# Moving four small copies to GpSimd, one normalisation ahead of a transposition, and splitting the last product: windowed attention with a gated MLP on one Trainium2 core

## The chip, the core and the metric

The kernel runs on one core of a Trainium2 chip. A core has a matrix engine (TensorE, in the profile PE, with its weight loads as PEld), a vector engine (VectorE, DVE), an activation engine (ScalarE, ACT), a general engine (GpSimd, POOL) and a queue engine (SyncE, SP), which here issues the DMAs. Each engine works through its own instructions in order and waits on semaphores for the others. Matrix products land in PSUM, all else lies in SBUF. The metric is the device time of one execution in microseconds (us).

## The reference

There are 8 batches, 8 heads, 576 positions and heads of 64. First comes attention in which each position sees itself and the 63 before it; then a gated MLP over the 512 joined columns, whose gate mixes positions.

```
scores = 0.125 * q @ k.T;  mask: 0 <= i - j < 64
attn   = softmax(scores) @ v             # then heads joined: x is (8, 576, 512)
h      = relu(x @ w_in);  u, v = h[..., :512], h[..., 512:]
v_n    = (v - mean(v)) / sqrt(var(v) + 1e-6)
v_s    = w_spatial @ v_n + b_spatial     # over positions
out    = (u * v_s) @ w_out               # float32
```

## The kernel before

The program is built of small named steps. Each step is a function that emits the instructions of one piece of work; a long string, `ORDER`, lists all steps in the order of emission, each with its engine (`DQ` is SP's DMA queue) and with the numbers of the buffers that it takes: `tk2_0:DVE:2`. Nothing else decides the order: an engine's instructions come in the order in which its steps stand in the list, and a step that waits holds up all that stands behind it on its engine. Semaphores between engines follow from which step writes and reads which part of a tile. PSUM has two pairs of banks (0 and 1) for scores and four single banks, which the list numbers 0 to 3 as well; a product can begin only when its bank has been read by the step that used it last.

A step's name has a letter or two, the batch, an underscore and what part of it. For batch b, head group g (0 or 1, four heads each) and half u of a group:

- `ldq`, `ldk`, `ldv`: loads by SP into the tiles nq, nk, nv. `cq`, `ck`: cast to float16 (hq, hk); on POOL three instructions of 384 columns. `tq`, `tk`: transposition by DVE (line 408) into qT, kT.
- `cv{b}_{g}{n}`: cast of V into hv (line 301 on POOL for batches 0 and 1, in two parts n = 0 and 1; from batch 2 on in one step with two instructions, line 299). P needs V at two offsets of 64 positions, so there is a second tile, hs, shifted by 64 partitions: `sl` copies the lower half of the partitions of hv to it, `su` the upper half, `s4` the last 64 positions from nv. These are the small copies of V; each is 64 partitions by 512 (256 for part 0 of `sl`).
- `S`: scores (line 470). `E`: exponential on ACT (477). `M`: the mask as a minimum on DVE (480, and 553 for the last 64 positions, marked r). `Z`: row sums as a product with ones (493). `N` and `n`: logarithm of the sum and exponential of its negative on ACT (519, 521), giving lz, the inverse. `P`: product with V from hv and hs (504). `X`: the normalisation, P's bank times lz, on DVE into x (512).
- `V` and `U`: the two halves of x @ w_in (643, 698; 656 and 703 for the last positions). `Vr`, `Ur`: relu on ACT (623, 711). `Vb`, `Va`: statistics on DVE (625, 627); `L1`, `L2`: inverse deviation on ACT (670, 672). `A`: v_n on DVE (682). `G`: product with w_spatial (728, 734). `Ge`: times u, on DVE (742). `O`: product with w_out (753). `Oe`: copy from the bank to ob by ACT (606). `st`: store by SP (610, 613, 616).
- `W`, `We`: transposition of w_spatial on PE (368) and the copy of it to SBUF; `cwo`, `cwin`, `cwsp`: casts of weights.

The batches are a pipeline: while batch 0 goes through the MLP, batch 1 is in attention and batch 2 is being loaded. The last 64 positions of out (`O{b}_4`) are computed beside `V{b+1}_4` (lines 656 and 659, in the two halves of the partitions of one bank); for batch 7 nothing follows, and line 765 computes them alone, in 64 partitions.

Of `ORDER`, around the change, DVE's steps read: su1_00, sl1_01, su1_01, A0_2, A0_1, We1, X1_00, tk2_0, su1_10, X1_01, Ge0_3, Ge0_4, tq2_0, su1_11, Ge0_2, X1_10, X1_11. PE's read: Z1_r, P1_01, P1_00, Z1_10, G0_4, G0_3, G0_0, G0_2, G0_1, P1_10, P1_11, S2_0, P1_r, V1_2. ACT's: N1_r, N1_10, n1_01, n1_10, sl1_10, cq2_0, sl1_11, n1_r, n1_11. POOL's: cv1_01, ck2_0, cv1_10, cv1_11, s41_1, ck2_1. Banks: P1_00 and G0_3 share bank 0, P1_01 and G0_2 bank 1, G0_4 and P1_10 bank 2.

Of the kernel before, what the change touches and what calls it, by code (L numbers as in the profile page):

```python
# [13 lines left out]
B = 8  # L14
# [26 lines left out]
Z1_11:PE:1 Ur0_1:ACT:2 A0_4:DVE ldq2_0:DQ:1 U0_0:PE:0 cwsp0:DVE E1_r0:ACT:1 E1_r1:ACT ldv1_12:DQ  # L41
A0_0:DVE:0 Ur0_4:ACT:3 A0_3:DVE:1 W0:PE:2 N1_11:ACT:1 ldv1_13:DQ cv1_00:DVE:2 W2:PE:3 M1_r:DVE
Ur0_0:ACT:4 cv1_01:POOL W3:PE:1 We0:DVE ldv1_14:DQ sl1_00:ACT:2 We2:DVE ldk2_1:DQ:4 W4:PE:0
s41_0:ACT su1_00:DVE We3:ACT sl1_01:DVE W1:PE:2 su1_01:DVE A0_2:DVE:2 We4:ACT Z1_r:PE:3 P1_01:PE:1
A0_1:DVE:3 N1_r:ACT:0 We1:DVE ck2_0:POOL:0 ldwo10:DQ:5 P1_00:PE:0 Z1_10:PE:3 X1_00:DVE:2 G0_4:PE:2
ldq2_1:DQ:7 N1_10:ACT:4 tk2_0:DVE:2 G0_3:PE:0 n1_01:ACT cv1_10:POOL:3 ldwo00:DQ:6 n1_10:ACT
sl1_10:ACT:3 G0_0:PE:3 su1_10:DVE X1_01:DVE cq2_0:ACT:1 ldwo11:DQ Ge0_3:DVE:0 G0_2:PE:1 ldwo01:DQ
Ge0_4:DVE:1 tq2_0:DVE:3 cv1_11:POOL ldq3_0:DQ:0 G0_1:PE:0 ldv2_00:DQ:0 s41_1:POOL sl1_11:ACT
su1_11:DVE n1_r:ACT Ge0_2:DVE:2 P1_10:PE:2 n1_11:ACT X1_10:DVE:3 ck2_1:POOL:2 P1_11:PE:1 ldk3_0:DQ:2
S2_0:PE:1:0 X1_11:DVE cwo10:ACT ldv2_01:DQ P1_r:PE:2 Ge0_0:DVE:3 V1_2:PE:1 E2_00:ACT:0 X1_r:DVE:1  # L50
Ge0_1:DVE:4 E2_01:ACT:1 V1_1:PE:3 cq2_1:POOL:3 ldv2_02:DQ tk2_1:DVE:0 V1_3:PE:2 Vr1_2:ACT:5
ldv2_03:DQ cwo00:POOL Vr1_1:ACT:6 tq2_1:DVE:1 U1_2:PE:0 ldv2_10:DQ:1 Vr1_3:ACT:7 cwo11:ACT
ldv2_11:DQ V1_0:PE:1 M2_00:DVE Ur1_2:ACT:5 Vb1_2:DVE:5 cwo01:ACT S2_1:PE:1:0 Vr1_0:ACT:4 M2_01:DVE
Z2_00:PE:3 cq3_0:POOL:0 ldv2_04:DQ E2_10:ACT:3 V1_4:PE:2 Vb1_1:DVE:1 ldv2_12:DQ Va1_2:DVE
Vb1_3:DVE:3 U1_1:PE:0 Vr1_4:ACT:2 M2_10:DVE Oe0_4:ACT:0 O0_0:PE:1 ck3_0:POOL:1 ldv2_13:DQ
Vb1_4:DVE:0 E2_11:ACT:2 Vb1_0:DVE:2 ldq4_0:DQ:3 O0_2:PE:2 Oe0_0:ACT:0 Va1_3:DVE ldv2_14:DQ Va1_4:DVE
Va1_1:DVE Ur1_1:ACT:0 Va1_0:DVE S2_r:PE:1:0 M2_11:DVE Z2_10:PE:1 cv2_00:POOL:1 ldv3_00:DQ:2
# [85 lines left out]
O6_1:PE:3 G7_2:PE:0 Oe6_1:ACT Oe6_3:ACT st6_0:DQ G7_0:PE:2 Ge7_2:DVE:6 st6_1:DQ st6_4:DQ G7_3:PE:3  # L143
Ge7_0:DVE:5 G7_1:PE:1 Ge7_3:DVE:7 U7_4:PE:0 Ge7_1:DVE:8 G7_4:PE:2 Ur7_4:ACT:2 O7_2:PE:3 Ge7_4:DVE:9
O7_0:PE:1 Oe7_2:ACT:1 st7_2:DQ O7_1:PE:0 Oe7_0:ACT:0 st7_0:DQ O7_3:PE:2 Oe7_1:ACT st7_1:DQ O7_4:PE:3
Oe7_3:ACT st7_3:DQ Oe7_4:ACT:0 st7_4:DQ
"""

NWARM = 25
# [20 lines left out]
class Plan:  # L170
# [3 lines left out]
    def add(self, name, engs, key, fn, deps=(), acq=(), uses=(), mode=None, nbytes=0, n=0):  # L174
        if isinstance(engs, tuple):
            engs = [engs]
        s = Step(name, engs, key, fn, deps, acq, uses, mode, nbytes, n)
        s.n = len(self.steps)
        self.steps.append(s)
        return s  # L180
# [17 lines left out]
def kernel(  # L198
# [11 lines left out]
    nc = tc.nc  # L210
# [55 lines left out]
    w_out_sb = [cpool.tile([128, 512], f16, name=f"wout{r}") for r in range(4)]  # L266
# [13 lines left out]
    def buf(tag, name):  # L280
        b = Buf(tag, name)
        if tag in SHAPES:
            shape, d = SHAPES[tag]
            b.make = lambda i: pool.tile(shape, d, tag=f"{tag}_{i}", bufs=1, name=name)
        return b

    plan = Plan()
    add = plan.add
# [309 lines left out]
    def out_steps(b, j, m, po, key, rows):  # L598
        half = j % 2
        if half == 0:  # L600
            OB[b] = (buf("ob", f"ob{b}_{j}") if j < 4 else buf("ob4", f"ob{b}_4")), None
        ob, first = OB[b]

        def view():
            return ob.t[rows, half, :] if j < 4 else ob.t[rows, :]
        cpy = add(f"Oe{b}_{j}", ("ACT", 0.49), key, lambda e: nc.scalar.copy(view(), m.t[rows, :]),  # L606
                  deps=[po, first], acq=[] if half else [ob], uses=[m] + ([ob] if half else []))
        OB[b] = ob, cpy
        if j == 4:
            add(f"st{b}_4", ("DQ", 0.45), key, lambda e: nc.sync.dma_start(  # L610
                out[b, 512:576, :], view()), deps=[cpy], uses=[ob], nbytes=0.4, n=64)
        elif b == B - 1:
            add(f"st{b}_{j}", ("DQ", 0.45), key, lambda e: nc.sync.dma_start(
                out[b, 128 * j:128 * j + 128, :], view()), deps=[cpy], uses=[ob], nbytes=0.72, n=128)
        elif half:
            add(f"st{b}_{j // 2}", ("DQ", 0.5), key, lambda e: nc.sync.dma_start(
                out[b, 128 * j - 128:128 * j + 128, :].rearrange("(f p) d -> p f d", f=2),
                ob.t[:, :, :]), deps=[cpy], uses=[ob], nbytes=1.42, n=256)
# [15 lines left out]
    def gmlp_steps(b, key):  # L634
        VS, ST, VN = [], [], []
        for j in range(4):
            m = buf("bank", f"pv{b}_{j}")
            vs = buf("vs", f"vs{b}_{j}")

            def emit_V(e, j=j, m=m):  # L640
                with nc.named_scope(f"V{b}_{j}"):
                    for r in range(4):
# [3 lines left out]
                     deps=[XD[b, r] for r in range(4)] + [WIN[1, r] for r in range(4)],  # L646
                     acq=[m], uses=[XB[b, 0], XB[b, 1]], mode="f")
            stat_steps(b, j, m, vs, pv, key + 0.1 + 0.03 * j, VS, ST)
        m = buf("bank", f"pv{b}_4")
# [25 lines left out]
        for j in range(5):  # L675
# [4 lines left out]
            def emit_A(e, j=j, jn=jn, vn=vn):  # L680
# [4 lines left out]
                          deps=[l2] + (GDONE.get(b - NSB, []) if j == 4 else []),  # L685
# [3 lines left out]
        for i in range(5):  # L689
            m = buf("bank", f"pu{b}_{i}")  # L690
            ru = buf("ru", f"ru{b}_{i}")
            n = 512 if i < 4 else 256

            def emit_U(e, i=i, m=m):
                with nc.named_scope(f"U{b}_{i}"):
# [4 lines left out]
                    else:  # L700
                        for c in range(4):
                            for r in range(4):
# [4 lines left out]
                     deps=[XD[b, r] for r in (range(4) if i < 4 else [4])]  # L707
                     + [WIN[0, r] for r in range(4)], acq=[m],
                     uses=[XB[b, 0], XB[b, 1]] if i < 4 else [XB[b, 4]], mode="f")
            RU.append((ru, add(f"Ur{b}_{i}", ("ACT", 0.06 + 0.00083 * n), key + 0.2 + 0.03 * i,  # L710
                               lambda e, m=m, ru=ru, n=n: nc.scalar.activation(  # L711
                                   ru.t[:, 0:n], m.t[:, 0:n], AF.Relu), deps=[pu], acq=[ru], uses=[m])))
        G = []
        gd = []
        for i in range(5):
            m = buf("bank", f"pg{b}_{i}")
            g = buf("g", f"g{b}_{i}")
            n = 512 if i < 4 else 256
            ru, rd = RU[i]

            def emit_G(e, i=i, m=m):
                def vk(kk):
                    return (VN[kk].t[:, :], 128) if kk < 4 else (vn4_t[b % NSB][:, :], 65)
                with nc.named_scope(f"G{b}_{i}"):
# [5 lines left out]
                    else:  # L730
                        for c in range(4):
                            for kk in range(5):
# [6 lines left out]
                     deps=AP + WSP, acq=[m], uses=[vn for vn in VN if vn], mode="f")  # L739
            gd.append(pg)  # L740
            G.append((g, add(f"Ge{b}_{i}", ("DVE", 0.07 + 0.00105 * n), key + 0.4 + 0.03 * i,
                             lambda e, m=m, g=g, ru=ru, n=n: nc.vector.tensor_tensor(  # L742
                                 g.t[:, 0:n], m.t[:, 0:n], ru.t[:, 0:n], ALU.mult),
                             deps=[pg, rd], acq=[g], uses=[m, ru])))
        GDONE[b] = gd
        G4[b] = G[4]
        for j in range(4):
            m = buf("bank", f"po{b}_{j}")

            def emit_O(e, j=j, m=m):  # L750
                with nc.named_scope(f"O{b}_{j}"):
                    for r in range(4):
                        nc.tensor.matmul(m.t[:, :], G[r][0].t[:, 128 * j:128 * j + 128],  # L753
                                         w_out_sb[r][:, :], start=(r == 0), stop=(r == 3))
            po = add(f"O{b}_{j}", ("PE", 0.866), key + 0.7 + 0.03 * j, emit_O,
                     deps=[G[r][1] for r in range(4)] + WOUT, acq=[m],
                     uses=[G[r][0] for r in range(4)], mode="f")
            out_steps(b, j, m, po, key + 0.7 + 0.03 * j, slice(0, 128))
        if b == B - 1:
            m = buf("bank", f"po{b}_4")  # L760

            def emit_O4(e, m=m):
                with nc.named_scope(f"O{b}_4"):
                    for r in range(4):
                        nc.tensor.matmul(m.t[0:64, :], G[4][0].t[:, 64 * r:64 * r + 64],
                                         w_out_sb[r][:, :], start=(r == 0), stop=(r == 3))
            po = add(f"O{b}_4", ("PE", 0.87), key + 0.69, emit_O4, deps=[G[4][1]] + WOUT, acq=[m],
                     uses=[G[4][0]], mode="v")
            out_steps(b, 4, m, po, key + 0.69, slice(0, 64))

    for i in range(NWARM):
        m = buf("bank", f"warm{i}")
# [8 lines left out]
    for b in range(B):  # L783
        for g in (0, 1):
            load_steps(b, g, (-1.0 + 0.1 * g) if b == 0 else b - 1.5 + 0.4 * g)
            att_steps(b, g, b + 0.36 * g)
        rem_steps(b, b + 0.72)
        gmlp_steps(b, b + 1.0)
# [40 lines left out]
```

## Time and profile before

| | us |
|---|---|
| median of three runs | 203.99 |
| lowest and highest of them | 203.55, 204.42 |
| the profiled execution, its own time | 204.42 |
| its span, first to last instruction | 202.6 |
| granted TensorE clock, mean | 0.999 |

| engine | busy, us | share of the span | instructions |
|---|---|---|---|
| PE | 189.1 | 93% | 2923 |
| ACT | 167.9 | 83% | 308 |
| DVE | 162.4 | 80% | 310 |
| POOL | 74.0 | 37% | 140 |

The DMAs move 42.69 MB in the span, 211 GB/s on the mean. Times within the span are counted from its first instruction. A row of the timeline gives the start, the length, the engine, the line, the operation, the tile written and the tiles read, and in brackets the idle time of the engine before it and what ended that. A row may join several like instructions that follow one another (x2 and so on). A row of the waits reads: who waited, for whom, microseconds in total, how often, the longest. The chain of work that ended last is followed back from the last instruction, at each step to what released it; its pieces give start, length, engine, tile and line.

### The profile page before, as it was taken

The numbers are of one execution on the slowest core, as the hardware profiler recorded it, in microseconds if no ns is written. First come the engines' busy times: TensorE is split into PE (matmuls) and PEld (weight loads), VectorE is DVE, ScalarE is ACT, GpSimd is POOL, SyncE is SP. The second block draws the span as 40 slices with busy tenths as digits, with TensorE's granted clock in tenths as the row PEclk, the third lists the DMA queues.
The fourth block names the chain that finished last, engine by engine and source line by source line (L and its number), as shares of the span: only waits on it lengthen the run. The fifth ranks groups of instructions, "written<-read, shape, count | busy, mean of one in ns | idle before, by whom it ended". The sixth has DMA issues, their size and how long they took to land.

```text
span 202.6 us, 6997 instructions
## 1 busy us (share of the span) xinstructions
PE 189.1 (93%) x2923; PEld 97.7 (48%) x2923; DVE 162.4 (80%) x310; ACT 167.9 (83%) x308; POOL 74.0 (37%) x140
## 2 busy tenths in 40 slices
PE   7578899889999999999999999999999999999992
PEld 2233535545455544664554545554465555444450
DVE  4599979999999899799699898979957795647420
ACT  2578899894999899997998999999999999467342
POOL 5202565364795298335847998000000000000000
PEclk9999999999999999999999999999999999999999
DMA  6997999999896947998978993996623003200445
GB/s 226 359 264 195 309 386 223 289 375 380 174 268 230 297 147 202 262 295 207 343 178 208 271 331 129 229 299 229 184 107 116 3 5 131 107 0 0 161 131 179
DMA packets 50195, 42.69 MB, mean 211 GB/s; under 512 B 39345, under 2 KB 39345, under 8 KB 50162
## 3 DMA queue, kind: packets, MB, share of 16 engines
q1 hardware_dynamic: 50162, 42.23, 69.8%
q8 instruction: 23, 0.38, 0.8%
q14 instruction: 10, 0.08, 0.1%
HBM read 32.79 MB, written 9.44 MB: 208 GB/s over the span
## 4 chain that ended last, share of the span: by engine, by line
PE 73%; DVE 10%; DMA 8%; ACT 3%; issue 2%; SPq 1%; POOL 1%; POOLq 0%; ACTq 0%
PE bank L728 15%; PE bank L753 14%; PE bank L643 12%; PE bank L698 11%; DMA nq<-in_q_dram 4%; PE pair L470 4%; PE bank L504 4%; PE bank L493 3%; DMA nk<-in_k_dram 3%; PE bank L656 3%; PE bank L734 2%; PE bank L703 2%; DVE qT L408 2%; DVE st L625 1%; DVE hs L301 1%
## 5 line engine op out<-in xcount | busy, mean ns | idle before, releaser
L728 PE MATMUL bank<-wspT,vn 128*128 128x512 f16 (+1 forms) x160 | 37.7, 379 | 0.3 <-DVE x L512 0.3
L477 ACT ACTIVATE e<-pair 128x1024 f16<-128x1024 f32 x32 | 31.9, 1027 | 4.1 <-PE pair L470 3.8
L742 DVE TENSOR_TENSOR g<-bank,ru 128x512 f16<-128x512 f32 (+1 forms) x40 | 24.9, 632 | 11.0 <-PE bank L728 5.0
L698 PE MATMUL bank<-x,win 128*128 128x512 f16 x128 | 31.6, 379 | 0.0
L753 PE MATMUL bank<-wout,g 128*128 128x512 f16 x128 | 31.3, 379 | 0.0
L643 PE MATMUL bank<-win,x 128*128 128x512 f16 x128 | 30.5, 379 | 0.0
L711 ACT ACTIVATE ru<-bank 128x512 f32<-128x512 f32 (+1 forms) x40 | 21.4, 561 | 8.4 <-PE bank L698 4.6
L625 DVE BATCH_NORM_STATS2 st<-vs 128x6 f32<-128x512 f16 (+1 forms) x40 | 25.9, 670 | 2.9 <-ACT vs L623 2.6
L606 ACT COPY ob<-bank 128x512 f32<-128x512 f32 (+1 forms) x40 | 23.2, 588 | 3.7 <-PE bank L753 3.1
L623 ACT ACTIVATE vs<-bank 128x512 f16<-128x512 f32 (+1 forms) x40 | 23.0, 596 | 3.0 <-PE bank L643 2.1
L512 DVE TENSOR_TENSOR x<-bank,lz 128x512 f16<-128x512 f32 x32 | 21.3, 683 | 4.9 <-PE bank L504 2.3
L728 PEld LDWEIGHTS <-vn 128*128 128x128 f16 (+1 forms) x160 | 14.9, 97 | 18.3 <-issue 1.0
L480 DVE TENSOR_TENSOR e<-e,mask 128x1024 f16<-128x1024 f16 x32 | 22.8, 729 | 1.0 <-ACT e L477 1.0
L296 POOL CAST hq<-nq 128x384 f16<-128x384 f32 x33 | 17.2, 560 | 13.0 <-DMA nq<-in_q_dram 11.5
L408 DVE STREAM_TRANSPOSE qT<-hq 128x576 f32<-128x576 f32 x16 | 19.8, 1245 | 2.7 <-POOL hq L296 2.3
L408 DVE STREAM_TRANSPOSE kT<-hk 128x576 f32<-128x576 f32 x16 | 19.9, 1244 | 1.2 <-ACT hk L293 0.9
L519 ACT ACTIVATE lz<-bank 128x512 f32<-128x512 f32 x32 | 18.5, 600 | 1.8 <-PE bank L493 1.7
L521 ACT ACTIVATE lz<-lz 128x512 f32<-128x512 f32 x32 | 19.6, 630 | 0.1
L643 PEld LDWEIGHTS <-x 128*128 128x128 f16 x128 | 11.9, 98 | 14.2 <-issue 0.4
L698 PEld LDWEIGHTS <-win 128*128 128x128 f16 x128 | 11.8, 98 | 14.4 <-issue 1.3
L296 POOL CAST hk<-nk 128x384 f16<-128x384 f32 x27 | 13.9, 551 | 12.9 <-DMA nk<-in_k_dram 10.5
L682 DVE TENSOR_SCALAR vn<-vs,mv,ln 128x512 f16<-128x512 f16 (+1 forms) x40 | 15.4, 434 | 3.7 <-ACT ln L672 3.6
(84 smaller groups left out, 290.7 us busy)
## 6 DMA issues: line engine op xcount, KB each, us to landing
nq<-in_q_dram SPq DMA_DIRECT2D x16, 576.0 KB, 5.9
nk<-in_k_dram SPq DMA_DIRECT2D x16, 576.0 KB, 5.6
nv<-in_v_dram SPq DMA_DIRECT2D x64, 128.0 KB, 5.1
out_dram<-ob SPq DMA_DIRECT2D x14, 512.0 KB, 4.3
wi<-in_moe_w_in_dram SPq DMA_DIRECT2D x8, 256.0 KB, 4.7
ws<-in_moe_w_spatial_dram SPq DMA_DIRECT2D x4, 288.0 KB, 8.6
nv<-in_v_dram SPq DMA_DIRECT2D x16, 64.0 KB, 3.3
wo<-in_moe_w_out_dram SPq DMA_DIRECT2D x4, 256.0 KB, 6.8
```

Source lines behind the costliest of these rows:

```text
L296: nc.gpsimd.tensor_copy(o[:, n:n + 384], i[:, n:n + 384])
L408: d = add(f"t{name}{b}_{g}", ("DVE", 1.09), key, lambda e: nc.vector.transpose(qt.t[:, :].rearrange("p (i j) -> p j i", j=18), h.t[:, :].b ...
L477: ex = add(f"E{b}_{g}{u}", ("ACT", 0.91), key, lambda e, u=u: nc.scalar.activation(e2[u].t[:, :, :], sc[u].t[:, :, :], AF.Exp, bias=0.0, s ...
L480: mins.append(add(f"M{b}_{g}{u}", ("DVE", 0.65), key, lambda e, u=u: nc.vector.tensor_tensor(e2[u].t[:, :, :], e2[u].t[:, :, :], mask[:, : ...
L606: cpy = add(f"Oe{b}_{j}", ("ACT", 0.49), key, lambda e: nc.scalar.copy(view(), m.t[rows, :]), deps=[po, first], acq=[] if half else [ob], ...
L623: rl = add(f"Vr{b}_{j}", ("ACT", 0.49), key, lambda e: nc.scalar.activation(vs.t[0:jn, :], m.t[0:jn, :], AF.Relu), deps=[pv], acq=[vs], us ...
L625: s1 = add(f"Vb{b}_{j}", ("DVE", 0.6), key + 0.02, lambda e: nc.vector.bn_stats(st6.t[0:jn, 0:6], vs.t[0:jn, :]), deps=[rl], acq=[st6], us ...
L643: nc.tensor.matmul(m.t[:, :], xr(b, r)[:, 128 * j:128 * j + 128], w_in_sb[r][:, 512:1024], start=(r == 0), stop=(r == 3))
L698: nc.tensor.matmul(m.t[:, :], w_in_sb[r][:, 128 * i:128 * i + 128], xr(b, r), start=(r == 0), stop=(r == 3))
L728: nc.tensor.matmul(m.t[:, :], w[0:kn, 128 * i:128 * i + 128], wspT[kk][0:kn, 0:512], start=(kk == 0), stop=(kk == 4))
L742: lambda e, m=m, g=g, ru=ru, n=n: nc.vector.tensor_tensor(g.t[:, 0:n], m.t[:, 0:n], ru.t[:, 0:n], ALU.mult),
L753: nc.tensor.matmul(m.t[:, :], G[r][0].t[:, 128 * j:128 * j + 128], w_out_sb[r][:, :], start=(r == 0), stop=(r == 3))
```

## The change

There are four edits.

- The small copies sl1_01, su1_01, su1_10 and su1_11 go from DVE to POOL, at the same places in the list.
- On DVE, X1_01 comes ahead of tk2_0 instead of behind it.
- The last product, O7_4, is computed as two halves of 256 columns: the first half into partitions 0 to 63 of the bank, the second into partitions 64 to 127, four matmuls each, in turn. Its copy Oe7_4 then has 128 partitions by 256 and is made by DVE. Its store is two stores of 64 rows by 256 columns, one issued by SP, one by ACT.
- The store st7_3 is issued by ACT instead of SP. ACT issues it right behind its last copy, Oe7_3, and the half store st7_41 after it.

```
-s41_0:ACT su1_00:DVE We3:ACT sl1_01:DVE W1:PE:2 su1_01:DVE A0_2:DVE:2 We4:ACT Z1_r:PE:3 P1_01:PE:1
+s41_0:ACT su1_00:DVE We3:ACT sl1_01:POOL W1:PE:2 su1_01:POOL A0_2:DVE:2 We4:ACT Z1_r:PE:3 P1_01:PE:1
...
-ldq2_1:DQ:7 N1_10:ACT:4 tk2_0:DVE:2 G0_3:PE:0 n1_01:ACT cv1_10:POOL:3 ldwo00:DQ:6 n1_10:ACT
-sl1_10:ACT:3 G0_0:PE:3 su1_10:DVE X1_01:DVE cq2_0:ACT:1 ldwo11:DQ Ge0_3:DVE:0 G0_2:PE:1 ldwo01:DQ
+ldq2_1:DQ:7 N1_10:ACT:4 G0_3:PE:0 n1_01:ACT X1_01:DVE tk2_0:DVE:2 cv1_10:POOL:3 ldwo00:DQ:6
+n1_10:ACT sl1_10:ACT:3 G0_0:PE:3 su1_10:POOL cq2_0:ACT:1 ldwo11:DQ Ge0_3:DVE:0 G0_2:PE:1 ldwo01:DQ
...
-su1_11:DVE n1_r:ACT Ge0_2:DVE:2 P1_10:PE:2 n1_11:ACT X1_10:DVE:3 ck2_1:POOL:2 P1_11:PE:1 ldk3_0:DQ:2
+su1_11:POOL n1_r:ACT Ge0_2:DVE:2 P1_10:PE:2 n1_11:ACT X1_10:DVE:3 ck2_1:POOL:2 P1_11:PE:1
...
-Oe7_3:ACT st7_3:DQ Oe7_4:ACT:0 st7_4:DQ
+Oe7_3:ACT st7_3:ACT Oe7_4:DVE:0 st7_40:DQ st7_41:ACT
...
+        n = 256 if (b, j) == (B - 1, 4) else 512
...
-            return ob.t[rows, half, :] if j < 4 else ob.t[rows, :]
-        cpy = add(f"Oe{b}_{j}", ("ACT", 0.49), key, lambda e: nc.scalar.copy(view(), m.t[rows, :]),
+            return ob.t[rows, half, :] if j < 4 else ob.t[rows, 0:n]
+        last = (b, j) == (B - 1, 4)
+        cpy = add(f"Oe{b}_{j}", ("DVE", 0.4) if last else ("ACT", 0.49), key,
+                  lambda e: (nc.vector.tensor_copy if last else nc.scalar.copy)(view(), m.t[rows, 0:n]),
...
-        if j == 4:
+        if j == 4 and b == B - 1:
+            for f, eng in enumerate(("DQ", "ACT")):
+                add(f"st{b}_4{f}", (eng, 0.45), key, lambda e, f=f: (nc.sync, nc.scalar)[f].dma_start(
+                    out[b, 512:576, 256 * f:256 * f + 256], ob.t[64 * f:64 * f + 64, 0:256]),
+                    deps=[cpy], uses=[ob], nbytes=0.2, n=64)
+        elif j == 4:
...
-            add(f"st{b}_{j}", ("DQ", 0.45), key, lambda e: nc.sync.dma_start(
+            q = ("ACT", nc.scalar) if j == 3 else ("DQ", nc.sync)
+            add(f"st{b}_{j}", (q[0], 0.45), key, lambda e: q[1].dma_start(
...
-                        nc.tensor.matmul(m.t[0:64, :], G[4][0].t[:, 64 * r:64 * r + 64],
-                                         w_out_sb[r][:, :], start=(r == 0), stop=(r == 3))
+                        for f in (0, 1):
+                            nc.tensor.matmul(m.t[64 * f:64 * f + 64, 0:256],
+                                             G[4][0].t[:, 64 * r:64 * r + 64],
+                                             w_out_sb[r][:, 256 * f:256 * f + 256],
+                                             start=(r == 0), stop=(r == 3))
...
-            out_steps(b, 4, m, po, key + 0.69, slice(0, 64))
+            out_steps(b, 4, m, po, key + 0.69, slice(0, 128))
```

More of the change, by code (lines that the diff above doesn't have):

```diff
@@ L43 @@
 Ur0_0:ACT:4 cv1_01:POOL W3:PE:1 We0:DVE ldv1_14:DQ sl1_00:ACT:2 We2:DVE ldk2_1:DQ:4 W4:PE:0
-s41_0:ACT su1_00:DVE We3:ACT sl1_01:DVE W1:PE:2 su1_01:DVE A0_2:DVE:2 We4:ACT Z1_r:PE:3 P1_01:PE:1
+s41_0:ACT su1_00:DVE We3:ACT sl1_01:POOL W1:PE:2 su1_01:POOL A0_2:DVE:2 We4:ACT Z1_r:PE:3 P1_01:PE:1
 A0_1:DVE:3 N1_r:ACT:0 We1:DVE ck2_0:POOL:0 ldwo10:DQ:5 P1_00:PE:0 Z1_10:PE:3 X1_00:DVE:2 G0_4:PE:2
-ldq2_1:DQ:7 N1_10:ACT:4 tk2_0:DVE:2 G0_3:PE:0 n1_01:ACT cv1_10:POOL:3 ldwo00:DQ:6 n1_10:ACT
-sl1_10:ACT:3 G0_0:PE:3 su1_10:DVE X1_01:DVE cq2_0:ACT:1 ldwo11:DQ Ge0_3:DVE:0 G0_2:PE:1 ldwo01:DQ
+ldq2_1:DQ:7 N1_10:ACT:4 G0_3:PE:0 n1_01:ACT X1_01:DVE tk2_0:DVE:2 cv1_10:POOL:3 ldwo00:DQ:6
+n1_10:ACT sl1_10:ACT:3 G0_0:PE:3 su1_10:POOL cq2_0:ACT:1 ldwo11:DQ Ge0_3:DVE:0 G0_2:PE:1 ldwo01:DQ
 Ge0_4:DVE:1 tq2_0:DVE:3 cv1_11:POOL ldq3_0:DQ:0 G0_1:PE:0 ldv2_00:DQ:0 s41_1:POOL sl1_11:ACT
-su1_11:DVE n1_r:ACT Ge0_2:DVE:2 P1_10:PE:2 n1_11:ACT X1_10:DVE:3 ck2_1:POOL:2 P1_11:PE:1 ldk3_0:DQ:2
[L50 to L54, printed above, removed]
+su1_11:POOL n1_r:ACT Ge0_2:DVE:2 P1_10:PE:2 n1_11:ACT X1_10:DVE:3 ck2_1:POOL:2 P1_11:PE:1
+ldk3_0:DQ:2 S2_0:PE:1:0 X1_11:DVE cwo10:ACT ldv2_01:DQ P1_r:PE:2 Ge0_0:DVE:3 V1_2:PE:1 E2_00:ACT:0
+X1_r:DVE:1 Ge0_1:DVE:4 E2_01:ACT:1 V1_1:PE:3 cq2_1:POOL:3 ldv2_02:DQ tk2_1:DVE:0 V1_3:PE:2
+Vr1_2:ACT:5 ldv2_03:DQ cwo00:POOL Vr1_1:ACT:6 tq2_1:DVE:1 U1_2:PE:0 ldv2_10:DQ:1 Vr1_3:ACT:7
+cwo11:ACT ldv2_11:DQ V1_0:PE:1 M2_00:DVE Ur1_2:ACT:5 Vb1_2:DVE:5 cwo01:ACT S2_1:PE:1:0 Vr1_0:ACT:4
+M2_01:DVE Z2_00:PE:3 cq3_0:POOL:0 ldv2_04:DQ E2_10:ACT:3 V1_4:PE:2 Vb1_1:DVE:1 ldv2_12:DQ Va1_2:DVE
 Vb1_3:DVE:3 U1_1:PE:0 Vr1_4:ACT:2 M2_10:DVE Oe0_4:ACT:0 O0_0:PE:1 ck3_0:POOL:1 ldv2_13:DQ
```

## The prediction

> **What bounds the kernel now.** I read four views in this order: the page's first part, who PE waited for (before and after 48 us), the chain of work that ended last, and the timelines of POOL and of the end. The span of the profiled execution is 202.6 us and its own time 204.42 us, so 1.82 us lie around the span; the median of the three runs shown is 203.99 us, 0.43 below the profiled one. My sum is a difference, taken off both. What a measurement of this kernel can tell from no change is about 0.5%, 1.02 us.
>
> ```profile
> PE 189.1 (93%) x2923; PEld 97.7 (48%) x2923; DVE 162.4 (80%) x310; ACT 167.9 (83%) x308; POOL 74.0 (37%) x140
> ```
>
> PE has the most work, but the share is an average. Who PE waited for, first in the stretch 36 to 48 us, then from 48 us to the end:
>
> ```profile
> PE bank L734 <- DVE wspT L301: 0.8, 1, 0.8
> PE bank L504 <- DVE g L742: 0.4, 1, 0.4
> PE bank L728 <- DVE x L512: 0.3, 1, 0.3
> ```
>
> ```profile
> PE pair L539 <- issue: 0.3, 1, 0.3
> ```
>
> After 48 us one wait of 0.3 us is all that the view shows of PE (shorter ones are not counted). So whatever moves PE's work at 48 us moves the end, unless a supply is late then. Ahead of it PE waits for DVE, and the chain runs on DVE without a break (start, us, engine, tile, line):
>
> ```profile
> 38.47 0.29 DVE hs L301
> ...
> 38.79 0.28 DVE hs L301
> ...
> 39.11 0.29 DVE hs L301
> ...
> 39.43 1.16 DVE vn L682 x2
> 40.59 0.36 DVE wspT L301
> 40.95 0.60 DVE x L512
> 41.55 1.17 DVE kT L408
> ...
> 42.75 0.73 DVE hs L301
> ...
> 43.51 0.69 DVE x L512
> 44.20 0.93 DVE g L742 x2
> 45.12 1.17 DVE qT L408
> ...
> 46.32 0.29 DVE hs L301
> ...
> 46.64 0.70 DVE g L742
> ...
> 47.38 0.44 PE bank L504 x16
> ```
>
> In order these are su1_00, sl1_01, su1_01; A0_2 and A0_1; We1; X1_00; tk2_0; su1_10; X1_01; Ge0_3 and Ge0_4; tq2_0; su1_11; Ge0_2; then P1_11 on PE. Four of the five hs copies leave, and X1_01 and tk2_0 change places. POOL in the same stretch has room between its casts:
>
> ```profile
> 37.56 0.63 POOL L301 CAST hv<-nv 128x512 f16<-128x512 f32 x1 [2.76 <-DMA nv<-in_v_dram]
> 39.43 1.53 POOL L296 CAST hk<-nk 128x384 f16<-128x384 f32 x3 [1.24 <-ACT wspT L293]
> 40.90 0.61 POOL L301 CAST hv<-nv 128x512 f16<-128x512 f32 x1
> 42.72 0.62 POOL L301 CAST hv<-nv 128x512 f16<-128x512 f32 x1 [1.20 <-DMA nv<-in_v_dram]
> ```
>
> And the end, where nothing runs beside the last product, copy and store:
>
> ```profile
> 197.55 1.05 PE L765 MATMUL bank<-wout,g 128*64 128x512 f16 x4
> 198.64 0.58 ACT L606 COPY ob<-bank 64x512 f32<-64x512 f32 x1 [0.40 <-PE bank L765]
> 199.25 0.47 SPq L610 DMA_DIRECT2D out_dram<-ob  x1
> ```
>
> **The change part by part: the copies and the moved normalisation.** DVE sheds sl1_01 and su1_01 (38.79 to 39.43: 0.64), su1_10 (42.72 to 43.48: 0.76, swollen, see below) and su1_11 (46.29 to 46.61: 0.32), together 1.72 us of the chain. That is the most that this part can give.
>
> POOL takes them at the price of its own rows: a copy hs of 64x512 takes 635 ns on average over 24 and 698 over the two of batch 0. cv1_01 ends at 38.19; two copies of 0.61 to 0.70 after it end at 39.43 to 39.65. I take 39.5, since two such copies later in the trace took 1.18 together (56.71 us). DVE finished su1_01 at 39.40, so P1_01 on PE, which reads these halves, is 0.1 late. Behind P1_01 on PE wait P1_00, Z1_10, G0_4; behind Z1_10 on ACT wait N1_10 (40.22), then n1_01 (40.71 to 41.34). All become 0.1 later. ck2_0, next on POOL, starts at 39.43 once its load is there; it slips by at most 0.2, and tk2_0, which needs it, now comes later anyway. su1_10 fits before the load at 42.72, su1_11 behind s41_1 (ends 43.73) before the next cast at 44.36; P1_10 and P1_11 need them at 45.5. No transfer is moved by this: the four copies read hv, not the loaded nv, so the queue of SP waits for none of them.
>
> Now DVE's own queue. Without the two copies A0_2 starts at 38.8, We1 and X1_00 follow 0.64 earlier, X1_00 ends at 40.9 (41.1 if the A's wait for POOL). X1_01 now stands next and waits for n1_01: until 41.44. So 0.4 to 0.5 of the 1.72 turns into a new wait, and behind it in DVE's queue stand tk2_0, Ge0_3, Ge0_4, tq2_0. X1_01 then ends at 41.47 + 0.69 = 42.16, where it ended at 44.20. From there to the end of Ge0_2 it was 3.13 (44.20 to 47.33); less su1_11 with its gap (0.35), plus tk2_0 (1.17), it is 3.95: 46.11 against 47.33, **1.22 earlier**. What these need is there: G0_3 follows X1_00, ck2_0 ends by 41.2, cq2_0 on ACT by 43.3, and G0_2, which waited 0.3 for X1_01 at 44.25, finds its bank free and ends at 44.4, before Ge0_2 at 45.4. P1_11, S2_0 and V1_2 follow as before, so the stream of PE from 48 us is 1.22 earlier. Bounds: 1.72 if n1_01 doesn't hold X1_01; 0.5 if each POOL copy takes 0.95, as a cast of POOL beside DVE's minimum e does (54.62 less 53.65): su1_01 ends 0.7 later than I took.
>
> At 42.75 the copy on DVE took 0.73 instead of 0.29: it stood until POOL's cast of 42.72 to 43.33 was over. The A's at 39.43 took 0.65 and 0.59 beside POOL's casts, against 0.72 for two at 36.32 without POOL. So the two engines do shut each other out, and the copies now lie on POOL beside su1_00 and the A's. The Trainium skill (SBUF — State Buffer, "Who interferes with whom") says that a copy or tensor_scalar of VectorE in a two-port mode and a GpSimd instruction exclude each other for a whole instruction, whoever is first; it says this in both directions, which speaks against the change. The trace agrees for DVE behind POOL; by the rule POOL would also stand behind su1_00 and an A, 0.29 and 0.40, and the gain here would be 0.5 instead of 1.2. I stay nearer the rows of 39.88 and 40.40, where POOL's casts beside the A's grew only from 0.51 to 0.57.
>
> **Does it last to the end?** What feeds PE after 48 us must come 1.22 earlier too. DVE has less to do, ACT stood idle 3.03 us before E2_00, so both follow. The loads are the doubt: DMA runs at 391 GB/s from 42 to 48 us. But the casts end well ahead of the transpositions that need them (q2_1: 48.35 against 51.16; q3_0: 52.22 against 58.35; q4_1: 72.95 against 74.89), and from 73.4 us on SP's loads queue behind stores that wait for ACT's copies (73.40, 80.06), so they move with the work. I take all of it as lasting.
>
> **The end.** The last product becomes eight matmuls of 256 columns into two halves of the partitions. At 54.05, 54.27, 54.48 and 54.70 us a matmul of line 656 and one of line 659, into different halves of one bank, start together, so four pairs of 512 columns took four steps of 0.216. Four pairs of 256 take 0.43 instead of 0.86: **0.43 earlier**; nothing, if they don't pair. DVE's copy of 128x256 f32: no such row; nearest is g 128x256 from a bank, 0.42, ends 0.29 (hs copy) and 0.69 (g 128x512). I take 0.40 against ACT's 0.58. DVE has been idle since 194.7 and the older stores that it waits for are long landed. So the data are ready at 198.62, 0.6 early. The two stores then go from SP (198.65) and from ACT. ACT's queue issues st7_3 first, at 198.28; if an issue costs it what it costs SP here (0.33 to 0.47), the half store goes out at 198.67 and lands as the last did, 2.24 later (2.0 to 2.2 for the others), at 200.9 against 201.49. One more queue to be waited for at the end costs a semaphore of 0.06. **0.5 earlier**; ends 0.9 (a copy of 0.29, landing in 2.05) and 0, if an issue on ACT takes 0.88, as one of SP did at 190.35. The Trainium skill (DMA: Bandwidth & Descriptors, "Issuing engines are not separate DMA queues") says that transfers from either queue run on the same 16 engines and a second issuer saves only issue time; by it the landing would be that of SP, as taken. No run here shows a store from ACT.
>
> **Sum.** 1.22 + 0.5 = 1.7: 204.42 to 202.7 for an execution like the profiled one, 203.99 to **202.3** in the median.
>
> **The rivals.** (1) POOL's copies are shut out by DVE, 0.95 each: the first part gives 0.5, the sum is 1.0, time 203.0, on the edge of what can be told. For it: casts of 0.95 to 1.07 beside the minima; against it: no minimum runs at 38 to 40 us. (2) The gain at 48 us is eaten by a load or a collision of DVE and POOL further on (at 118.25 a minimum of er took 1.67 instead of 0.41), and only the end remains: 203.5. Against it: the slack above. (3) Slower: stores from ACT's queue, which this trace never uses, land late. With the first part as forecast the last issue is due at 197.45 (198.67 less 1.22) and its landing at 199.7. To end 1.02 later than before, it must land at 202.5 (201.49 + 1.02): from 5.05 after its issue on the kernel is slower beyond doubt. Loads under full traffic take 5.9 from issue to landing; that price gives 203.35 against 201.49, a time of 205.9. Against it, the five last stores of SP land in 2.0 to 2.2, and there is hardly any other traffic then.
>
> **How the numbers follow.** Forecast 0.60 (201.4 to 202.9), rival 1 0.12, rival 2 0.13, rival 3 0.09, other 0.06. Faster by over 0.5%: 0.60, half of rival 1 and half of the other, 0.69. Within 0.5%: rival 2, half of rival 1 and a sixth of the other, 0.20. Slower: rival 3 and a third of the other, 0.11. Range: from both parts' best (1.72 + 0.9: 201.4) to both at nothing (204.0), which leaves out rival 3 and little else.
>
> **What would show it.** POOL's two copies end by 39.7; DVE waits about 0.4 for ACT's lz ahead of X1_01; Ge0_2 ends near 46.1 and PE goes on without waits from 46.2; nothing for PE after that; the last product takes some 0.6 instead of 1.05; the last store is issued near 198.7 less 1.2. I am wrong if POOL's copies take 0.9 each, if PE shows waits after 48 us that it had not, or if the ACT store lands more than 3 us after its issue.

## The result, and the profile after

The changed kernel takes 202.8 us in the median of 20 runs, against 204.13 us for the kernel before in 20 runs beside it, 1.3 us less. The ratios given here, with 95% intervals in brackets, leave out the executions that took over 1.5% more than the fastest of their kernel. This one is 0.9944 [0.9919, 0.9969], that is 0.56% or 1.1 us faster. The forecast was 202.3 us, 1.7 us below the 203.99 us known then. The profiled execution took 202.82 us with a span of 201.0, so 1.82 us lie around the span, as before.

The first part of the page of the changed kernel (busy time, share of the span, instructions):

```profile
PE 188.6 (94%) x2927; PEld 97.7 (49%) x2927; DVE 161.2 (80%) x307; ACT 167.0 (83%) x307; POOL 76.5 (38%) x144
```

PE's own work is 0.5 us less, nearly all of it in the last product. POOL has 2.5 us more, DVE 1.2 us less. To see where time went I cut both spans at three instructions: M1_r, the last step of DVE that stands ahead of everything that the change touches (line 553); V1_2, with which PE's unbroken stream begins (line 643, in the changed kernel 653); and O7_4, the last product (line 765, now 776). These are the windows of the kernel before (window, its length, then busy time of PE, PEld, DVE, ACT and POOL with their instructions, granted clock, DMA share, GB/s):

```profile
37.30:48.70 11.40, 9.74 (x200) 5.98 (x199) 11.15 (x22) 7.34 (x15) 6.90 (x14) 1.00 1.03 357
48.70:197.55 148.85, 148.39 (x2205) 76.88 (x2200) 120.12 (x225) 131.27 (x246) 53.29 (x96) 1.00 0.63 183
197.55:202.60 5.05, 1.05 (x5) 0.36 (x4) 0.00 (x0) 1.17 (x2) 0.00 (x0) 0.95 0.50 176
```

And of the changed kernel, cut at the same instructions:

```profile
36.50:46.76 10.26, 9.47 (x199) 6.00 (x199) 9.61 (x18) 7.64 (x16) 7.60 (x14) 1.00 1.02 350
46.76:196.50 149.74, 148.56 (x2202) 76.87 (x2201) 120.31 (x225) 130.91 (x246) 54.78 (x99) 1.00 0.64 186
196.50:201.00 4.50, 0.60 (x9) 0.33 (x8) 0.42 (x1) 0.58 (x1) 0.00 (x0) 0.82 0.56 196
```

The first stretch, below called the stage, is 1.1 us shorter; DVE was busy for 98% of it (11.15 of 11.40) and is now for 94% (9.61 of 10.26). The end is 0.5 shorter. The middle is 0.9 longer, although PE's work in it is the same. And M1_r, which the change doesn't touch, began 0.8 earlier. The two numbers that I had forecast are there; two others, of nearly their size, stand beside them and had to be explained.

Whom PE waited for in the changed kernel, from 36 to 52 us and then to the end:

```profile
PE bank L744 <- DVE wspT L301: 0.4, 1, 0.4
PE bank L504 <- POOL hs L301: 0.2, 1, 0.2
PE bank L653 <- DVE x L512: 0.2, 1, 0.2
```

```profile
PE bank L562 <- DVE g L752: 0.6, 1, 0.6
PE pair L539 <- issue: 0.5, 1, 0.5
```

Before V1_2 the wait for We1 (tile wspT) halved and those for Ge0_2 (g) and X1_01 went; waits of 0.2 for POOL's copies and for X1_11, ahead of V1_2, are new. The wait at line 562 (Z of the last positions) was not there before. The chain of the changed kernel through the stage (start, length, engine, tile, line):

```profile
37.69 0.53 DVE hs L301
...
38.25 1.12 DVE vn L692 x2
...
39.42 0.46 DVE wspT L301
...
39.91 0.76 PE bank L744 x20
40.67 4.33 PE bank L738 x20
45.01 0.39 PE bank L504 x16
...
45.42 0.28 DVE x L512
...
46.03 0.69 DVE x L512
```

These are su1_00, the two A steps and We1 on DVE; then on PE, without a gap, G0_4, the other four G and P1_10; then X1_10 and X1_11 on DVE, for which V1_2 waits. It isn't the chain that I had drawn: X1_01, tk2_0, the Ge steps and tq2_0 are not in it. From 39.9 to 45.4 us the limit is PE itself. What POOL and DVE did there, in the two timelines:

```profile
36.62 0.78 POOL L301 CAST hv<-nv 128x512 f16<-128x512 f32 x1 [2.01 <-DMA nv<-in_v_dram]
37.46 1.28 POOL L301 COPY hs<-hv 64x512 f16<-64x512 f16 x2
```

```profile
40.71 0.69 DVE L512 TENSOR_TENSOR x<-bank,lz 128x512 f16<-128x512 f32 x1 [0.25 <-ACT lz L521]
...
45.42 1.29 DVE L512 TENSOR_TENSOR x<-bank,lz 128x512 f16<-128x512 f32 x2 [0.33 <-PE bank L504]
```

The two copies take 1.28 us on POOL with the gap between them, 0.61 each. DVE's su1_00 beside them takes 0.53 instead of 0.29. X1_01 waits 0.25 for n1_01, and later X1_10 waits 0.33 for PE. The end of the changed kernel, in its timeline:

```profile
196.47 0.63 PE L776 MATMUL bank<-wout,g 128*64 128x256 f16 x8
...
197.20 0.38 ACTq L623 DMA_DIRECT2D out_dram<-ob  x1
197.20 0.42 DVE L610 COPY ob<-bank 128x256 f32<-128x256 f32 x1 [3.58 <-ACT ob L610]
197.65 0.47 SPq L615 DMA_DIRECT2D out_dram<-ob  x1
197.66 0.55 ACTq L615 DMA_DIRECT2D out_dram<-ob  x1
```

The product takes 0.63 instead of 1.05, the copy 0.42 instead of 0.58. Both half stores go out together; that of SP lands 1.9 us after its issue, that of ACT 2.3, so ACT's ends the work.

### The profile page after: what moved, and what is told of

It reads as the page before. It is cut to its first block, busy times and chain, and to the rows that moved or that the text cites. A ratio compares the mean times of both kernels' runs of the same rounds, so it can differ in the third digit from the quotient of the medians.

```text
span 201.0 us, 7008 instructions
## 1 busy us (share of the span) xinstructions
PE 188.6 (94%) x2927; PEld 97.7 (49%) x2927; DVE 161.2 (80%) x307; ACT 167.0 (83%) x307; POOL 76.5 (38%) x144
## 4 chain that ended last, share of the span: by engine, by line
PE 70%; DMA 9%; SPq 7%; ACT 5%; DVE 5%; POOL 1%; issue 1%; POOLq 0%
PE bank L738 16%; PE bank L653 12%; PE bank L763 12%; PE bank L708 10%; DMA nk<-in_k_dram 9%; SPq L422 4%; PE pair L470 4%; PE bank L504 3%; PE bank L666 3%; PE bank L493 3%; PE bank L744 2%; SPq L327 2%; ACT e L477 1%; PE bank L713 1%; ACT ob L610 1%
## 5 line engine op out<-in xcount | busy, mean ns | idle before, releaser
L610 ACT COPY ob<-bank 128x512 f32<-128x512 f32 (+1 forms) x39 | 22.6, 588 | 3.3 <-PE bank L763 3.1
L296 POOL CAST hq<-nq 128x384 f16<-128x384 f32 x33 | 16.5, 536 | 13.1 <-DMA nq<-in_q_dram 12.5
L763 PEld LDWEIGHTS <-g 128*128 128x128 f16 x128 | 11.8, 98 | 13.4 <-issue 0.5
```

The lines of the kernel that those rows point to most:

```text
L610: lambda e: (nc.vector.tensor_copy if last else nc.scalar.copy)(view(), m.t[rows, 0:n]),
```

## The experiments

The theory to begin with was that of the prediction, with one addition after the first profile: the stage and the end gain what was forecast, and some of it is lost again in the middle, where the load of K for batch 4 now came late. The rivals were that the middle differs by chance from execution to execution, and that only one of the two parts is worth anything. The experiments ran in three groups, each on one chip beside its own runs of the kernel before, and each has one profile.

### Each part alone, and the changed kernel again

`copies` has the edits in the order list around V of batch 1 and keeps the old end. `tail` has the new end and keeps the old copies and order.

```diff
 copies:
-... sl1_01:DVE ... su1_01:DVE ... tk2_0:DVE:2 ... su1_10:DVE X1_01:DVE ... su1_11:DVE
+... sl1_01:POOL ... su1_01:POOL ... X1_01:DVE tk2_0:DVE:2 ... su1_10:POOL ... su1_11:POOL
 tail:
-Oe7_3:ACT st7_3:DQ Oe7_4:ACT:0 st7_4:DQ
+Oe7_3:ACT st7_3:ACT Oe7_4:DVE:0 st7_40:DQ st7_41:ACT
```

Expected of `copies`:

> The kernel before with the four copies on POOL and X1_01 ahead of tk2_0; the end as before. Theory: the stretch from su1_00 to V1_2 (first matmul of line 643) shrinks by 1.2 us (10.3 before, 9.07 in the changed kernel), some of it is lost again near 87 us where PE waits for DVE behind a late nk4_1, and the end is unchanged; time 0.4 to 1.2 below before, ratio 0.994 to 0.998. Rival A (all of the gain is from the end): ratio 1.000, and PE's work ahead of the last product ends no earlier. Rival B (nothing is lost near 87 us): ratio 0.994, PE's wait there under 0.1.

Expected of `tail`:

> The kernel before with the new end alone: last product in halves, copied by VectorE, two stores, st7_3 from ACT. Theory: from the first matmul of the last product to the last landing 3.5 us as in the changed kernel, where before it took 3.94: 0.45 below before, ratio 0.9978. Rival A: the end carries the whole difference, 1.1 below before, ratio 0.9944. Rival (the new queue costs something outside the span): ratio 1.000 or above with the span 0.4 shorter.

Expected of the changed kernel itself, run again beside these two (`after_again`):

> The changed kernel once more, beside the others. Theory (its loss near 87 us is regular, since the load of nk4_1 has no slack left once the work is earlier): PE waits again 0.5 to 0.8 us there for DVE, with ACT waiting about 1 us for nk4_1; ratio 0.993 to 0.996. Rival (a chance of that one execution): no wait of PE there, span near 200.3, ratio nearer to 0.992.

On one chip, with the kernel before at 204.59 us: `copies` 203.35 us, ratio 0.9936 [0.9903, 0.9969]; `tail` 204.25 us, 1.0014 [0.9975, 1.0053]; the changed kernel 202.67 us, 0.9892 [0.9855, 0.9929]. The edits around V carry the gain that whole times can resolve. The half microsecond of the end would be a ratio of 0.9975, at the edge of the interval of `tail`: whole times don't show it, and its profile does (table further down). The median of `tail` came out above that of the kernel before, as its last rival said, but the cost outside the span that this rival needs isn't there: time less span is 1.8 us, as in the other profiles. Neither `copies` nor `after_again` shows the wait at line 562, so the theory of a regular loss near 87 us failed in both, and their rivals (no wait there) held; `after_again` has a shorter middle too. The chain of `after_again` through the stage is another one (the same columns):

```profile
40.00 0.60 ACT lz L519
40.60 0.53 ACT lz L521
...
41.15 0.69 DVE x L512
41.84 1.17 DVE kT L408
43.01 0.85 DVE g L752 x2
43.85 1.15 DVE qT L408
45.01 0.53 DVE g L752
...
45.58 0.44 PE bank L504 x16
```

That is the chain that the prediction drew: N1_10 and n1_01 on ACT, X1_01, tk2_0, Ge0_3 and Ge0_4, tq2_0, Ge0_2, P1_11. V1_2 begins at the same point of the stage with it (10.22 us after M1_r, against 10.25 in the first profile). In this execution ACT had stood 0.6 us for a load of V ahead of We3 and We4, so N1_10 and n1_01 came later. The two chains are within some tenths of each other, and an execution shows the one or the other.

### Was the loss in the middle made by the change?

In the first profile of the changed kernel the waits between 80 and 90 us read:

```profile
ACT hk L293 <- DMA nk<-in_k_dram: 1.0, 1, 1.0
...
DVE kT L408 <- ACT hk L293: 0.7, 1, 0.7
PE bank L562 <- DVE g L752: 0.6, 1, 0.6
```

The load of K landed late, ACT cast it late, DVE stood in tk4_1 and PE behind DVE. `early_k4` is the changed kernel with this load ahead of a store in SP's queue:

```diff
-... n3_01:ACT st1_4:DQ Va2_3:DVE Vb2_4:DVE:1
-O1_3:PE:0 n3_00:ACT ldk4_1:DQ:6 sl3_00:POOL:3
+... n3_01:ACT ldk4_1:DQ:6 st1_4:DQ Va2_3:DVE Vb2_4:DVE:1
+O1_3:PE:0 n3_00:ACT sl3_00:POOL:3
```

> The changed kernel with the load of nk4_1 one place earlier in SP's queue, ahead of the store st1_4 that waits for ACT. Theory (the late nk4_1 takes 0.75 us of the gain): it is issued 1.6 us earlier, ACT's and DVE's waits at 84 to 86 us go, PE's wait of 0.6 at 87 goes, time 0.5 to 0.75 below the changed kernel, ratio to before 0.990 to 0.992. Rival (the wait near 87 comes from the shift itself, whatever is late): another wait takes its place and the time is that of the changed kernel, ratio 0.9944.

It took 203.47 us, ratio 0.9936 [0.989, 0.9982], no better than the changed kernel beside it. Its middle has no wait of 0.2 or more at line 562 and is 149.3 us long all the same. The theory fell: the late load was a chance of one execution. `before_again`, the kernel before with one more profile, says the same from the other side:

> The kernel before once more, for its profile. The stretch from the first hs copy of VectorE to V1_2 was 10.23 us in the first profile and 9.85 with the same code there (new end alone). Theory (the difference is chance: su1_10 on VectorE meets a POOL cast or doesn't): again between 9.8 and 10.3; from V1_2 to the last product 148.5 to 149.7. Rival (10.23 is the rule): 10.2 to 10.3.

It took 204.14 us. The stretch from the first hs copy to V1_2 was 9.98 us, within the theory's range; that from V1_2 to the last product was 150.77, over a microsecond outside it. After 49 us PE stands in a wait that no other profile has:

```profile
PE bank L698 <- ACT vs L623: 1.5, 1, 1.5
```

ACT had stood 1.8 us there for POOL's hv. So the middle loses 0 to 2 us, in other places each time, with the old code as with the new. The three stretches of all profiles but those of two experiments further down, worked out from the starts of the three instructions:

| profile | M1_r begins | stage | middle | end | span |
|---|---|---|---|---|---|
| before | 37.30 | 11.40 | 148.85 | 5.03 | 202.6 |
| before_again | 35.40 | 11.15 | 150.77 | 5.03 | 202.3 |
| order_only | 36.74 | 11.07 | 149.05 | 5.03 | 201.9 |
| tail | 36.88 | 11.02 | 149.41 | 4.48 | 201.8 |
| copies | 36.73 | 10.28 | 149.34 | 5.03 | 201.4 |
| pool_only | 36.07 | 10.21 | 149.52 | 5.03 | 200.8 |
| the changed kernel | 36.51 | 10.25 | 149.71 | 4.51 | 201.0 |
| after_again | 36.67 | 10.22 | 148.51 | 4.51 | 199.9 |
| early_k4 | 37.51 | 10.21 | 149.34 | 4.52 | 201.6 |
| tail_sp | 37.11 | 10.22 | 149.19 | 5.09 | 201.6 |
| we1_act | 37.16 | 9.94 | 149.29 | 4.49 | 200.9 |

The stage falls into two groups with nothing between them: 11.02 to 11.40 with the four copies on DVE (mean 11.16), 10.21 to 10.28 with them on POOL (mean of six 10.23; `we1_act`, with a further edit, is shorter still), a difference of **0.93 us**. No run moves fewer than all four, so how the 0.93 divides among the copies is not shown. The middle is 149.5 in the mean of the first four rows and 149.3 in that of the six: nothing is lost there regularly. The end is 0.51 to 0.55 shorter wherever it is new and both queues are used.

### The copies or the order?

`pool_only` moves the four copies and leaves X1_01 behind tk2_0; `order_only` does the reverse.

```diff
 pool_only:
-... sl1_01:DVE ... su1_01:DVE ... su1_10:DVE ... su1_11:DVE
+... sl1_01:POOL ... su1_01:POOL ... su1_10:POOL ... su1_11:POOL
 order_only:
-... tk2_0:DVE:2 G0_3:PE:0 n1_01:ACT ... su1_10:DVE X1_01:DVE
+... G0_3:PE:0 n1_01:ACT X1_01:DVE tk2_0:DVE:2 ... su1_10:DVE
```

> The kernel before with the four copies on POOL alone; X1_01 stays behind tk2_0, the end as before. The stretch counted is from the first hs copy of VectorE to V1_2: 10.23 us before, 9.05 to 9.11 in the four profiles with both edits. Theory (VectorE's work counts, not its order, since PE goes through the five G without a wait either way): 9.05 to 9.2. Rival (the forecast's reading, in which X1_01's place decides when G0_2 gets its bank): 9.4 to 9.9, and PE waits for VectorE ahead of the third or fourth G.

> The kernel before with X1_01 ahead of tk2_0 alone; all copies on VectorE. Theory (the order moves no work off VectorE): stretch from the first hs copy to V1_2 10.1 to 10.3, as before; PE's wait of 0.3 ahead of G0_2 goes and comes back ahead of P1_11. Rival (the order gives a part of the gain): 9.9 or less.

`pool_only` took 202.85 us against 203.66, ratio 0.9946 [0.9909, 0.9983]; `order_only`, in one run, 203.59. In the table the first has the whole gain of the stage and the second none. By the stretch named beforehand `pool_only` has 9.04, as the theory said, but `order_only` has 9.88, which its rival had claimed for itself. That bound was badly chosen: `tail` and `before_again`, both with the old order, have 9.85 and 9.98. PE's waits in the stage, for `order_only`:

```profile
PE bank L734 <- DVE wspT L301: 0.7, 1, 0.7
...
PE bank L504 <- DVE g L742: 0.5, 1, 0.5
```

The wait of G0_2 for X1_01 (0.3 before) is gone, and P1_11 then waits for Ge0_2: what PE saves in one place it stands for in the next. For `pool_only`:

```profile
PE bank L734 <- DVE wspT L301: 0.4, 1, 0.4
PE bank L504 <- POOL hs L301: 0.2, 1, 0.2
PE bank L643 <- DVE x L512: 0.2, 1, 0.2
```

They are those of the changed kernel to the tenth. In `pool_only` Ge0_2 ends 8.20 us after M1_r begins (43.59 and 0.68, less 36.07), in the changed kernel 8.58 (44.41 and 0.68, less 36.51). So the new order even costs DVE 0.4, and V1_2 doesn't come later for it, because X1_10 waits for PE in both.

### How much room have POOL's copies, and who else could take work from DVE?

`pool_twice` is the changed kernel with each of sl1_01 and su1_01 made twice on POOL. `su_act` gives su1_00, the copy left on DVE, to ACT. `we1_act` gives We1 to ACT, behind N1_r.

```diff
 pool_twice:
-lambda e, l0=l0, hi=hi: cp(e, hs.t[0:64, l0:hi, :, :], hv.t[0:64, l0:hi, :, :]),
+lambda e, l0=l0, hi=hi, n=n: [cp(e, hs.t[0:64, l0:hi, :, :], hv.t[0:64, l0:hi, :, :])
+                              for _ in range(2 if (b, g, n) == (1, 0, 1) else 1)],
 su_act:
-s41_0:ACT su1_00:DVE We3:ACT
+s41_0:ACT su1_00:ACT We3:ACT
 we1_act:
-A0_1:DVE:3 N1_r:ACT:0 We1:DVE
+A0_1:DVE:3 N1_r:ACT:0 We1:ACT
```

> The changed kernel with each of sl1_01 and su1_01 done twice on POOL, one after the other; the output is the same. Theory (POOL's two copies are just short of the path: P1_01, Z1_10 and G0_4 stand behind them on PE): 1.25 us more on POOL moves G0_4 by 0.8 to 1.0, stretch to V1_2 9.9 to 10.1, PE waits for POOL's hs some 1.3 us longer. Rival (POOL has room to spare): under 9.3.

`pool_twice` took 204.50 us in one run, and its stage is 12.52 us long, 2.27 more than that of the changed kernel, for 1.34 us more on POOL (2.62 for four copies, 1.28 for two). Its chain:

```profile
36.29 1.10 POOL hv L301
...
37.45 0.62 POOL hs L301
...
38.12 0.61 POOL hs L301
...
38.78 0.61 POOL hs L301
...
39.48 0.60 POOL hs L301
...
40.12 0.75 PE bank L506 x20
40.87 0.43 PE bank L495 x2
41.30 1.18 PE bank L746 x20
```

The lines are two higher here. POOL's copies now release P1_01 and P1_00 (L506), then come Z1_10 (L495), G0_4 and the others. G0_4 begins 4.73 after M1_r, 1.33 later than in the changed kernel, where I had expected 0.8 to 1.0, and the other 0.94 is lost behind it. Not all of this is the price of the copies, for in this execution TensorE's granted clock was halved for 3.4 us of the stage (a window as above; the third number from the end is the clock):

```profile
39.80:43.20 3.40, 3.08 (x45) 2.09 (x46) 1.52 (x4) 1.86 (x5) 3.20 (x7) 0.51 1.09 359
```

In every other profile it is 1.00 throughout the stage. The five G products took 6.03 us here from the first to the last, and 5.09 in the changed kernel: that is the 0.94. And from the end of POOL's last copy to G0_4 it took 1.15 us, against 0.71 in `we1_act` (below), where G0_4 follows POOL's copies as well. At that pace G0_4 would begin 0.9 later than in the changed kernel, which is an estimate, and what I had expected. So the copies have little room: of the 2.27 us some 0.9 is the price of 1.34 more on POOL, and the rest, by this estimate, is the clock. PE had stood 1.1 us for POOL just before; whether that lowered the clock is not shown (a wait of 1.5 us in `before_again` left it at 1.00).

> The changed kernel with su1_00 on ACT as well, so that no hs copy of batch 1 is left on VectorE ahead of A0_2. Theory (in the changed kernel G0_4 waits for We1 on VectorE, behind su1_00 of 0.53 and the two A): We1 ends 0.4 to 0.55 earlier, V1_2 0.3 to 0.5 earlier counted from M1_r (VectorE, line 553), time 0.3 to 0.5 below the changed kernel. Rival (the next wait takes it: X1_01 for ACT's n1_01, or P1_01 for POOL): V1_2 under 0.15 earlier.

`su_act` took 203.17 us, ratio 0.9977 [0.9941, 1.0013]; its stage is 10.94, 0.69 longer than in the changed kernel where 0.3 to 0.5 less was expected. DVE gains even more than was expected: We1 ends 2.45 after M1_r begins instead of 3.35. But on ACT the copy stands ahead of We3 and We4, ACT had stood 0.4 us for a load of V before it, and PE waits for We3 and We4:

```profile
PE bank L504 <- ACT wspT L293: 0.9, 1, 0.9
```

> The changed kernel with We1 on ACT, behind N1_r, in a gap that ACT had. Theory (all G wait for We1, which in the changed kernel is VectorE's last of four): G0_4 0.4 to 0.5 earlier counted from M1_r, then Ge0_2 holds P1_11, V1_2 0.2 to 0.4 earlier (9.85 to 10.05 from M1_r, where it was 10.21 to 10.28). Rival (ACT is late, as with su1_00 there: N1_10 and n1_01 slip): V1_2 at 10.2 or later.

`we1_act` took 202.62 us against 204.58, ratio 0.9898 [0.9831, 0.9964]. G0_4 begins 0.46 earlier (2.94 instead of 3.40 after M1_r), V1_2 0.3 earlier. It is the shortest stage of all. By its time it can't be told from the changed kernel, whose two ratios are 0.9944 and 0.9892.

### The second queue at the end

`tail_sp` is the changed kernel with the last three stores all issued by SP:

```diff
-Oe7_3:ACT st7_3:ACT Oe7_4:DVE:0 st7_40:DQ st7_41:ACT
+Oe7_3:ACT st7_3:DQ Oe7_4:DVE:0 st7_40:DQ st7_41:DQ
```

> The changed kernel with its three last stores all issued by SP, the last two one after the other. From the first matmul of the last product to the end of the span it took 4.51 to 4.52 us with ACT's queue, 5.03 in the kernel before. Theory (a second issuer saves one issue of SP, 0.33 to 0.55): 4.7 to 5.0. Rival (ACT's issue, 0.55, and its later landing cost as much as they save): 4.4 to 4.6.

It took 203.32 us in one run. The end is 5.09 us long, outside both ranges, and 0.06 more than with the old product, copy and single store: without ACT's queue the halves are worth nothing. Its timeline:

```profile
196.38 1.20 SPq L623 DMA_DIRECT2D out_dram<-ob  x2
...
197.25 0.42 DVE L610 COPY ob<-bank 128x256 f32<-128x256 f32 x1 [3.58 <-ACT ob L610]
198.01 1.11 SPq L615 DMA_DIRECT2D out_dram<-ob  x2
```

SP issues st7_3 until 197.58. The data are ready at 197.67, but the first half store goes out at 198.01 and the second some 0.5 later, where in the changed kernel both go out at 197.65. The pause is no chance of this execution. In all six profiles in which SP issues four stores in a row, its next instruction begins 0.35 to 0.36 us after the fourth issue ends, against 0.05 after the others. In the kernel before that is 198.96, after 198.60, and the copy, which ended at 199.22, hid it. What SP does in the pause the traces don't say, and I leave it open.

## Why the prediction was right or wrong

**The copies on POOL: right.** The two copies were to end 2.2 after M1_r begins (39.5 less 37.30) and ended at 2.23 (37.46 and 1.28, less 36.51). P1_01 was to be 0.1 late and waited 0.2. Rival 1, POOL shut out at 0.95 a copy, fell: they took 0.61.

**The lock between DVE and POOL: there, but small.** su1_00 takes 0.53 beside POOL's copies, in this profile and in all others that have su1_00 on DVE and the four copies on POOL, where I had left it at 0.29. That is 0.24 on the way to We1, and nearly the whole price of the lock that the change brings: POOL's copies stay at 0.61, the two A steps take 0.96 to 1.28 with them and took 1.01 to 1.21 without, and POOL's cast ahead of them, which I had at 0.63, takes 0.65 to 1.11 in the other three profiles with the copies on DVE, so it is stretched with both codes. The Trainium skill (SBUF — State Buffer, "Who interferes with whom") says that either engine may shut out the other for a whole instruction. The trace agrees for DVE behind POOL (su1_00 ends 0.14 after POOL's first copy, as su1_10 ended 0.14 after POOL's cast before). For the other direction, the price that I had worked out by that rule, POOL's copies standing behind su1_00 and an A and a gain of 0.5 instead of 1.2, isn't seen: the gain was 1.15 against that profile.

**The new wait of X1_01: there, and not the limit.** I forecast 0.4 to 0.5 of waiting for n1_01 and the end of X1_01 at 4.86 after M1_r (42.16 less 37.30). It waited 0.25, and ended at 4.89. Ge0_2 was to end at 8.81 and ended at 8.58. The step that failed is the next one, "P1_11, S2_0 and V1_2 follow as before": the five G products, behind We1, end at 8.50 in this profile, so DVE's path and PE's are as good as tied, and X1_10 waits 0.33 for P1_10. V1_2 came at 10.25 after M1_r, where the forecast makes 10.18 (11.40 less 1.22). That it came so near is in part luck: Ge0_2 was 0.23 earlier than forecast, and the way from it to V1_2 was 0.30 longer (1.67 instead of 1.37). In `after_again` the forecast path did hold. With the failed step falls the edit of the order, which I had taken as the way to the gain: `order_only` and `pool_only` show that it gives nothing in the stage. The upper bound of 1.72 reckoned with DVE's path alone.

**The size of the stage: mis-sized by 0.3.** Forecast 1.22. Against the one profile that I had, 1.15; against four profiles with the copies on DVE, 0.93. Of the difference 0.24 is the profile itself: it is the longest of the four (11.40 against a mean of 11.16). One chance in it I had seen and yet counted whole, su1_10 at 0.73: in `tail` and `order_only` the same copy takes 0.29. A collision that depends on when a load lands is no fixed term of a sum.

**The end: right.** Forecast 0.5, measured 0.52. The product is 0.42 shorter (forecast 0.43); the copy takes 0.42 on DVE (0.40); ACT issued st7_3 in 0.38, between the bounds of 0.33 and 0.47; its half store landed 2.29 after issue (2.24). Rival 3, late landing from ACT's queue, fell. The sentence of the Trainium skill (DMA: Bandwidth & Descriptors, "Issuing engines are not separate DMA queues") that a second issuer saves only issue time stands: the store from ACT lands no sooner after its issue than that of SP. But at the end of the kernel nothing hides it. Of the 0.58 us between `tail_sp` and the changed kernel, 0.53 is the first half store's issue, behind which SP's second one stands, and 0.31 SP's pause; 0.25 goes the other way, since the last landing came 2.04 after its issue on SP and 2.29 on ACT.

**Does it last: right, but not seen in one profile.** Rival 2 was that a load eats the gain. By the sign that I had named, waits of PE after 48 us that were not there before, the first profile spoke for it (0.6 at line 562, and a middle 0.9 longer). `copies`, `after_again` and `early_k4` don't have this wait, and `before_again` loses more with the old code, so it was a chance of one execution. A middle that differs by up to 2 us from profile to profile could still hide a loss of a few tenths.

**The sum.** 0.93 and 0.52 make 1.45 us, 0.71% of 204.13. That lies in both intervals of the changed kernel, 0.31 to 0.81% and 0.71 to 1.45% (in the second at its edge). The forecast of 1.7, 0.83%, lies just outside the first and inside the second. The range of 201.4 to 204.0 held.

## What to carry to other kernels

Work on an engine that is busy through a whole stage is worth moving, but only down to the next chain: follow that one to the same end point as well, here We1 and five G products on PE, before an edit of the order is given credit. A copy moved to a slow engine must be checked for what stands behind it: doubling POOL's two copies, 1.3 us more on POOL, made the products on PE later by an estimated 0.9, and a halved clock in that execution took the other 1.4 of the 2.3 lost. So look at the granted clock of a stretch before its length is put down to an edit. And one profile has chances of half a microsecond to two in it; cut spans at instructions that the change doesn't touch, and compare stretches over several profiles.

## What the runs showed that I had not expected

- Stretches that the change doesn't touch differ between profiles of the same code: M1_r began at 37.30 and 35.40 in two of the kernel before, and the middle was 148.85 and 150.77. The span of the changed kernel was 201.0 and 199.9.
- PE pauses for 0.3 to 0.7 us within the matmuls of line 539 (541 in `pool_twice`) with no releaser shown ("issue") in most profiles, but not in `after_again`, `su_act`, `we1_act` or `tail_sp`. What it waits for there is not settled.
- SP pauses for 0.35 to 0.36 us after four stores in a row. In the kernel before the last copy hid this; in `tail_sp` the first half store left 0.34 us after its data were ready.
- In one execution (`pool_twice`) the granted clock was 0.51 from 39.8 to 43.2 us. What lowered it is not settled.
